# Five sums of the mixture ahead of the turn of raw K in VectorE's written order

## The chip, the cores and the metric

One core of one Trainium2 chip. The metric is the device time of one execution in microseconds; the time of a kernel is the median of its runs. Five engines work side by side, each through its own queue in order: TensorE (PE; its weight loads are shown apart as PEld), VectorE (DVE), ScalarE (ACT), GpSimd (POOL) and SyncE (SP), whose queue starts nearly all transfers.

## What is computed

Two blocks. The first is a recurrence over 768 time steps for 4 batches of 8 heads of dimension 40:

```python
for t in range(S):
    y[:, :, t] = np.einsum('bhd,bhde->bhe', rt, state)
    Sa = np.einsum('bhde,bhe->bhd', state, at)
    state_decay = state * wt[:, :, None, :] - np.einsum('bhd,bhe->bhde', Sa, bt)
    state = state_decay + np.einsum('bhd,bhe->bhde', vt, kt)
```

The second takes y as a matrix x of 3072 x 320 through four experts, with weights `p` normalised over the experts:

```python
for e in range(E):
    h = np.maximum(x @ w1[e], 0.0)
    out += p[:, e:e + 1] * (h @ w2[e])
```

All numbers are fp32; `w1[e]` is 320 x 1024, `w2[e]` 1024 x 320.

## The kernel before

**Units and steps.** Time is cut into 12 chunks of 64 steps, the batches into two pairs, which gives 24 units (`NU`). The main loop (line 1311) runs over `u` from 1 to 23; "step u" below is one pass of it. Three stages of different units overlap in a step: `step` of unit u (the state), `merge` and the first part of `step` for unit u + 1, `within` and `substitute` for unit u + 2.

**The chain of a unit.** `within` turns the raw inputs with VectorE (`turn_raw`, line 324): W into G, A into AT, R into RT, B into NT, K into KT. From unit 8 on (`BY_CHANNEL`), NT and KT are each turned in two halves, noted as `Br` and `Kr`, and then multiplied by `gp`, the reciprocal of the decays (lines 633 to 645; noted as `N` and `K`). NT is read by the matmuls `pfe`, KT by `pe`. `substitute` solves a triangular system: VectorE makes M, GpSimd works through it in the tile Z (lines 760 and 777). `merge` turns Z on VectorE into `Qc` and `QTc` (lines 793, 794), and TensorE then computes `pY` and `pQ`. In `step`, the matmuls `prn`, `psat`, `pxr` and `pdy` follow; VectorE adds Y (line 913) and the states (lines 924, 925) from `pdy`, and SP sends Y into `xT`, the input of the mixture.

**The mixture.** For each chunk of 128 x 2 rows and each expert, `ups` computes `ph = xT . w1` in two halves (`up_last`, `up_main`), and ScalarE writes relu of it into `hs` (line 978). The product with `w2` is done with sums of blocks: `add_h` (line 1096) makes five sums of blocks of `hs`, named a1, a7, a5, a2, a6 and noted as `sum_a0`, `sum_a1` and so on. Each is one VectorE addition of 128 x 512 (line 1104) into a tile of which there is only one. `down_1` computes `p431`: two terms of 8 matmuls from `hs`, a third of 8 from a1. `down_2` computes `p75` (from a7, a5) and `p26` (from a2, a6), 16 matmuls each. VectorE adds each result into `osb` (line 993): `p431` takes four adds, `p75` and `p26` two each. `ph` and the `p` tiles share one pool of three PSUM tiles in turn, so that a `p431` takes the tile that the `p26` before it held.

The pieces of the mixture stand in a list (`todo`), from which `mix` puts some between the parts of each step. In a late step TensorE sees in this order: `p75`, `p26`, `pev`, `pdy`, the start of a `ph`, `p431`, the rest of `ph`, `pg`, `pc`, `pY`, `prn`; later `p75`, `p26`, `pfe`, and `p431`, `pe`, `pxr`.

**What sets the order.** TensorE's order is the order of the program. VectorE's is made by the scheduler under stated dependences that cost no wait (`BEHIND`): the text `VECTOR_ORDER` for the early units, and rules in `ahead_of_merge` (lines 1441 to 1450) for units 8 to 23. A pair `(one, then)` in it means: `then` stands behind `one` on VectorE (line 1453):

```python
for one, then in [*zip(names, names[1:]), ..., *ahead_of_merge]:
    tc.add_manual_dep(made[then].ins, made[one].ins.name, BEHIND, ...)
```

In a late step ten sums are made: five behind the reciprocal `1/gp` (line 1449), and five, `sum_a{10 * (u - 1) - 50}` to the fourth after it, which line 1443 puts behind the multiplies `K` and `N` of unit u. These multiplies belong to the step u - 2; there are sixteen such groups, in steps 6 to 21.

Of the kernel before, what the change touches and what calls it, by code (L numbers as in the profile page):

```python
# [33 lines left out]
def kernel(  # L34
# [48 lines left out]
    NU = NC * B // 2  # L83
# [128 lines left out]
    BY_CHANNEL = 8  # L212
# [1222 lines left out]
    for piece in last:  # L1435
# [4 lines left out]
    waits_of_scalar = [(f"SXc0.{n}", "RTc1.0") for n in range(4)]  # L1440
    ahead_of_merge = [(f"{x}{u}", f"Qc{u - 1}") for u in range(BY_CHANNEL, NU) for x in "KN"]
    ahead_of_merge += [
        (f"{x}{u}", f"sum_a{10 * (u - 1) - 50 + n}") for u in range(BY_CHANNEL, NU) for x in "KN" for n in range(5)
    ]
    ahead_of_merge += [(f"VC{u}.{r}", f"1/gp{u + 1}") for u in range(BY_CHANNEL, NU - 1) for r in range(2)]
    ahead_of_merge += [(f"RH{u - 1}.{r}", f"1/gp{u + 1}") for u in range(BY_CHANNEL, NU - 1) for r in range(2)]
# [37 lines left out]
```

## Time and profile before

| | |
|---|---|
| time, median of 3 runs (lowest to highest) | 1082.37 us (1082.31 to 1082.71) |
| profiled execution, its own time | 1082.07 us |
| its span (first to last instruction) | 1080.3 us |
| TensorE busy / its weight loads | 1053.6 us / 944.2 us |
| VectorE busy | 801.6 us, 1565 instructions |
| GpSimd busy | 527.6 us, 1322 instructions |
| ScalarE busy | 344.2 us, 942 instructions |
| mean granted TensorE clock | 0.998 |

In the rows below, a timeline row gives the start, the duration, the engine, the line, the operation, output<-input, shapes and how many instructions were merged into the row; a bracket gives the idle time of the engine just before it and what ended it. A row of waits reads: who waited, for whom, total us, how many times, the longest.

### The profile page before, as it was taken

The page shows a single profiled execution, that of the slowest core. Times are in us where ns is not written, and L with a number is a line of the kernel's source. Part 1 is how long each engine was busy: PE and PEld are TensorE (multiplying, and loading weights), DVE is VectorE, ACT ScalarE, POOL GpSimd, SP SyncE. Part 2 cuts the span into 40 slices and gives each one's busy share as a digit, 9 for nine tenths or more (in the row PEclk, how much of TensorE's full clock was granted, in tenths as well). Part 3 has the DMA queues.
Part 4 walks back from the last instruction along what each step waited for, and adds up shares of the span by engine and source line. Part 5 has one row for each costly group of instructions (what it writes and reads, how often), then busy time and mean ns, then how long its engine had stood idle before and what let it go on. Part 6 is the DMA issues. An engine that isn't in the chain of part 4 may idle for free.

```text
span 1080.3 us, 38526 instructions
## 1 busy us (share of the span) xinstructions
PE 1053.6 (98%) x16022; PEld 944.2 (87%) x16022; DVE 801.6 (74%) x1565; ACT 344.2 (32%) x942; POOL 527.6 (49%) x1322
## 2 busy tenths in 40 slices
PE   8999999999999999999999999999999999999998
PEld 7888878888889989889989898998988998998887
DVE  7787679898777967978778779778787786634343
ACT  3433344423333323324233333232233333221110
POOL 6117777756465374464563653744735636420000
PEclk9999999999999999999999999999999999999999
DMA  6776644444444443543453353354444443121220
GB/s 119 192 202 140 138 106 112 83 101 106 109 96 109 102 113 74 131 108 78 114 126 82 88 143 71 92 133 88 99 113 101 102 104 86 53 73 51 75 85 13
DMA packets 275350, 111.05 MB, mean 103 GB/s; under 512 B 229816, under 2 KB 254952, under 8 KB 275176
## 3 DMA queue, kind: packets, MB, share of 16 engines
q1 hardware_dynamic: 271192, 107.75, 42.8%
q8 instruction: 126, 2.06, 0.8%
q10 hardware_dynamic: 3984, 0.84, 0.4%
q14 instruction: 48, 0.39, 0.1%
HBM read 100.65 MB, written 3.93 MB: 97 GB/s over the span
## 4 chain that ended last, share of the span: by engine, by line
PE 76%; DVE 10%; POOL 8%; issue 2%; DMA 2%; ACT 1%; SPq 1%; DVEq 0%; POOLq 0%
PE ph L110 33%; PE p L110 25%; POOL Z L777 5%; POOL Z L760 3%; PE pdy L110 2%; DVE a L1104 2%; PE prn L110 2%; PE po L110 2%; PE pxr L110 2%; PE psat L110 2%; PE pfe L110 1%; PE warm L110 1%; PE pc L110 1%; PE pY L110 1%; PE pe L110 1%
## 5 line engine op out<-in xcount | busy, mean ns | idle before, releaser
L777 POOL TENSOR_TENSOR Z<-Z 128x31 f32<-128x31 f32 (+7 forms) x704 | 261.1, 371 | 55.1
L110 PE MATMUL ph<-xT,w1b 128*128 128x256 f32 (+3 forms) x1536 | 222.4, 374 | 0.5 <-issue 0.5
L978 ACT ACTIVATE hs<-ph 128x512 f32<-128x512 f32 (+1 forms) x208 | 117.0, 564 | 331.8 <-PE ph L110 329.8
L110 PE MATMUL ph<-xT,w1a 128*128 128x256 f32 (+3 forms) x1536 | 220.8, 373 | 0.0
L993 DVE SCALAR_TENSOR_TENSOR osb<-p,gate,osb 128x320 f32<-128x320 f32 (+1 forms) x243 | 108.2, 482 | 133.1 <-PE p L110 130.9
L760 POOL TENSOR_TENSOR Z<-M,Z 128x62 f32<-128x62 f32 (+7 forms) x352 | 149.6, 425 | 95.3 <-DVE M L746 69.6
L110 PEld LDWEIGHTS ph<-xT,w1b 128*128 128x128 f32 (+1 forms) x1536 | 168.8, 161 | 27.8 <-issue 7.0
L110 PEld LDWEIGHTS ph<-xT,w1a 128*128 128x128 f32 (+1 forms) x1536 | 167.9, 161 | 28.3 <-issue 6.7
L1104 DVE TENSOR_TENSOR a<-hs 128x512 f32<-128x512 f32 x220 | 148.8, 710 | 41.2 <-ACT hs L978 41.2
L110 PE MATMUL p<-sums,a 128*128 128x160 f32 x1056 | 165.7, 300 | 9.7 <-DVE a L1104 9.7
L110 PEld LDWEIGHTS p<-sums,a 128*128 128x128 f32 x1056 | 152.6, 190 | 13.6 <-DVE a L1104 11.4
L727 POOL COPY below<-F 32x256 f32<-32x256 f32 x48 | 20.6, 430 | 177.4 <-ACT F L670 175.8
L110 PEld LDWEIGHTS p<-w,hs 128*128 128x128 f32 x704 | 98.6, 190 | 9.0 <-issue 7.8
L110 PE MATMUL p<-w,hs 128*128 128x160 f32 x704 | 104.9, 302 | 0.5 <-DVE osb L993 0.5
L110 PE MATMUL p<-w,a 128*128 128x160 f32 x704 | 102.8, 299 | 0.0
L110 PEld LDWEIGHTS p<-w,a 128*128 128x128 f32 x704 | 98.0, 190 | 0.0
L800 POOL COPY QT<-QTc 32x256 f32<-32x256 f32 x96 | 40.3, 420 | 92.6 <-DVE QTc L794 74.9
L898 ACT COPY RS<-pxr 64x256 f32<-64x256 f32 x88 | 32.3, 367 | 104.7 <-DVE SX L499 92.6
L582 DVE RECIPROCAL gp<-G 128x512 f32<-128x512 f32 x16 | 53.6, 3353 | 0.5
L730 DVE STREAM_TRANSPOSE M<-blocks 128x1024 f32<-128x1024 f32 x24 | 47.4, 1975 | 3.3 <-ACT blocks L722 3.0
L708 ACT COPY EV<-pev 64x160 f32<-64x160 f32 x96 | 23.1, 286 | 83.7 <-PE pev L110 83.4
L670 ACT COPY F<-pfe 128x256 f32<-128x256 f32 x48 | 15.5, 376 | 80.1 <-PE pfe L110 77.9
(167 smaller groups left out, 1422.0 us busy)
## 6 DMA issues: line engine op xcount, KB each, us to landing
w1a<-in_moe_w_dram SPq DMA_DIRECT2D x37, 512.0 KB
w1b<-in_moe_w_dram SPq DMA_DIRECT2D x37, 512.0 KB
w<-in_moe_w_dram SPq DMA_DIRECT2D x4, 1280.0 KB
w1a<-in_moe_w_dram SPq DMA_DIRECT2D x74, 64.0 KB
w1b<-in_moe_w_dram SPq DMA_DIRECT2D x74, 64.0 KB
out_dram<-osb SPq DMA_DIRECT2D x45, 80.0 KB
rawW<-in_w_dram SPq DMA_DIRECT2D x48, 72.0 KB
natV<-in_v_dram SPq DMA_DIRECT2D x42, 80.0 KB
```

What stands on the lines that cost most here:

```text
L110: return stated(nc.tensor.matmul(**k))
L582: pin(noted(nc.vector.reciprocal(out=gp[:], in_=G[:, :, 1:L + 1]), "1/gp", q.u))
L708: nc.scalar.copy(out=of_slot(q.EV[half(p)], i ^ p)[:, :, 0:D], in_=pev[i][half(p)])
L727: tc.keep_in_program_order(nc.gpsimd.tensor_copy(out=q.below[quarter(i)], in_=q.F[quarter(i), :, 0:Q]))
L730: ins = nc.vector.transpose(out=M[:], in_=cols)
L760: ins = eng.tensor_tensor(out=Z[:, 1:3, 0:n, j + 1:Q], in0=M[:, j:j + 2, None, j + 1:Q].to_broadcast([P, 2, n, m]), in1=Z[:, here, 0:n, j: ...
L777: eng.tensor_tensor(out=z[:, 0], in0=z[:, 0], in1=z[:, x], op=ALU.add)
L800: ins = nc.gpsimd.tensor_copy(out=q.QT[quarter(i), :, quarter(i % 2)], in_=QTc[quarter(i)])
L898: nc.scalar.copy(out=RS[half(s), x ^ s::2], in_=prs[x][half(s)].rearrange("p (j i) t -> p j i t", i=2),)
L978: ins = nc.scalar.activation(out=h[:, i * HF // 2:(i + 1) * HF // 2, 0:n], in_=ph[i][:], func=ACTF.Relu,)
L993: ins = nc.vector.scalar_tensor_tensor(out=to, in0=p, scalar=sc, in1=to, op0=ALU.mult, op1=ALU.add)
L1104: ins = nc.vector.tensor_tensor(out=t[:], in0=x, in1=y, op=op)
```

## The change

One rule of VectorE's order is replaced. Before, each of the five sums stood behind the multiplies K and N of unit u; now each of them stands ahead of `Kr{u}.0`, the turn of the first half of raw K of unit u. The tie to N is dropped.

```diff
     ahead_of_merge += [
-        (f"{x}{u}", f"sum_a{10 * (u - 1) - 50 + n}") for u in range(BY_CHANNEL, NU) for x in "KN" for n in range(5)
+        (f"sum_a{10 * (u - 1) - 50 + n}", f"Kr{u}.0") for u in range(BY_CHANNEL, NU) for n in range(5)
     ]
```

On TensorE, ScalarE, GpSimd and SP the instructions stand in the same order as before. On VectorE the scheduler's order moves with the rule. In step 9, for one, it was

```
RT turn, osb<-p75 (2), NT turns (2), NT multiply, osb<-p26 (2), Y (2), states and Y, KT turns, KT multiply, a1, a7, a5, a2, a6, osb<-p431 (4)
```

and becomes

```
RT turn, a1, a7, osb<-p75, a5, osb<-p75, a2, NT turn, osb<-p26, a6, osb<-p26, NT turn, NT multiply, Y (2), states and Y, KT turns, KT multiply, osb<-p431 (4)
```

In even steps the sums stand among the `osb` adds in the same way, and the KT turns and multiply come between them and Y, where before the sums came between KT and Y.

## The prediction

> **What bounds the kernel now.** I read the page's first part, then the waits of TensorE (PE) and of its weight loads (PEld) from 322 to 915 us.
>
> ```profile
> span 1080.3 us, 38526 instructions
> PE 1053.6 (98%) x16022; PEld 944.2 (87%) x16022; DVE 801.6 (74%) x1565; ACT 344.2 (32%) x942; POOL 527.6 (49%) x1322
> ...
> PE p L110 <- DVE a L1104: 9.7, 7, 1.4
> PE pY L110 <- DVE QTc L794: 1.0, 3, 0.5
> PE pY L110 <- PE pc L110: 0.7, 3, 0.2
> PE pY L110 <- issue: 0.2, 1, 0.2
> PEld p L110 <- DVE a L1104: 11.4, 7, 1.7
> ```
>
> TensorE is the bound: a change can gain only where TensorE stands still. In this stretch, which holds steps 8 to 21, it does so at two places: seven times before `p` for the A sums (`a`), and seven times before `pY`. The timeline of TensorE in step 8, then in step 9, shows both:
>
> ```profile
> 350.92 2.44 PE L110 MATMUL p<-w,hs 128*128 128x160 f32 x16
> 353.20 1.25 PE L110 MATMUL p<-sums,a 128*128 128x160 f32 x8
> 354.29 3.62 PE L110 MATMUL ph<-xT,w1a 128*128 128x256 f32 x16
> 358.27 0.69 PE L110 MATMUL pc<-RT,VT 40*64 40x64 f32 x32
> 359.18 0.59 PE L110 MATMUL pY<-QTc,below 64*64 64x64 f32 x13 [0.21 <-DVE QTc L794]
> ...
> 392.89 2.44 PE L110 MATMUL p<-w,hs 128*128 128x160 f32 x16
> 396.68 1.35 PE L110 MATMUL p<-sums,a 128*128 128x160 f32 x8 [1.35 <-DVE a L1104]
> 397.87 3.62 PE L110 MATMUL ph<-xT,w1a 128*128 128x256 f32 x16
> 401.85 0.69 PE L110 MATMUL pc<-RT,VT 40*64 40x64 f32 x32
> 402.37 0.57 PE L110 MATMUL pY<-QTc,below 64*64 64x64 f32 x13
> ```
>
> Step 8 goes from the start of `p431` (16 matmuls, then 8 that need sum a1) to the next `ph` in 354.29 - 350.92 = 3.37 us; step 9 takes 397.87 - 392.89 = 4.98. The stall costs 1.61, more than its 1.35 of idle time, because the pipeline fills anew. The weight loads' row gives all seven together: 11.4 us. At `pY` it is the even step that loses: 0.91 us from `pc` to `pY` against 0.52, so 0.39.
>
> The timeline of VectorE in the same two steps shows why:
>
> ```profile
> 345.79 0.55 DVE L993 SCALAR_TENSOR_TENSOR osb<-p,gate,osb 128x320 f32<-128x320 f32 x1 [3.23 <-PE p L110]
> 347.96 0.55 DVE L993 SCALAR_TENSOR_TENSOR osb<-p,gate,osb 128x320 f32<-128x320 f32 x1 [1.20 <-PE p L110]
> 350.25 3.66 DVE L1104 TENSOR_TENSOR a<-hs 128x512 f32<-128x512 f32 x5
> 353.83 0.74 DVE L913 TENSOR_TENSOR Y<-pdy,RS 128x256 f32<-128x256 f32 x2
> ...
> 387.76 0.55 DVE L993 SCALAR_TENSOR_TENSOR osb<-p,gate,osb 128x320 f32<-128x320 f32 x1 [4.16 <-PE p L110]
> 388.35 0.38 DVE L993 SCALAR_TENSOR_TENSOR osb<-p,minus_gate,osb 128x160 f32<-128x160 f32 x1
> 388.65 0.76 DVE L324 STREAM_TRANSPOSE NT<-rawB 128x256 f32<-128x256 f32 x2
> 389.44 0.69 DVE L640 SCALAR_TENSOR_TENSOR NT<-NT,gp 128x512 f32<-128x512 f32 x1
> 392.15 0.76 DVE L913 TENSOR_TENSOR Y<-pdy,RS 128x256 f32<-128x256 f32 x2 [1.13 <-PE pdy L110]
> 395.90 3.19 DVE L1104 TENSOR_TENSOR a<-hs 128x512 f32<-128x512 f32 x5
> 399.02 1.58 DVE L993 SCALAR_TENSOR_TENSOR osb<-p,gate,osb 128x320 f32<-128x320 f32 x4
> ```
>
> VectorE is idle for 3.23 us ahead of 345.79 and 4.16 ahead of 387.76, while work stands queued behind it. In step 9 the K work ends up behind Y and the states, and the sums behind K: they start at 395.90, though `p431` wants the first at 392.89 + (353.20 - 350.92) = 395.17. In step 8 they are in time, but push Y to 353.83 and the chain Y, states, `Qc`, `QTc` into `pY`.
>
> **The change part by part.** No instruction is added or removed; the order on TensorE, ScalarE, GpSimd and SP's queue is the same as before. On VectorE the five sums now stand, in sixteen steps (6 to 21), between and ahead of the four `osb` adds of `p75` and `p26`; K's turns and multiply come behind them.
>
> *The sums' new place.* The sums need `hs`, whose second half ScalarE finishes here, and four of their tiles must have been read by the expert before:
>
> ```profile
> 343.61 0.60 ACT L978 ACTIVATE hs<-ph 128x512 f32<-128x512 f32 x1 [1.13 <-PE ph L110]
> 385.58 0.60 ACT L978 ACTIVATE hs<-ph 128x512 f32<-128x512 f32 x1 [0.76 <-PE ph L110]
> ```
>
> So sums can begin at 344.21 and 386.18. At 3.66/5 = 0.73 each, the first two are done at 345.67 and 387.64, inside the idle time, and the first `osb` add starts no later. The others alternate with the adds, by when `p75` and `p26` have read their tiles. Hence a1 is ready some 8 us ahead of 395.17 and the stall goes whole: **-11.4 us**. If only its visible idle time came back: -9.7; if a1 were still late, 0.
>
> *What is behind the sums in step 9.* From 387.76: add 0.55, sum 0.73, add 0.38, sum 0.73, half of the NT turns 0.38, add 0.55, sum 0.73, add 0.38 end at 392.19. That frees the PSUM tile of `p26`, which `p431` takes at 392.89: 0.7 to spare (in step 8, 349.84 against 350.92). Then 0.38 + 0.69 of NT: Y starts at 393.26 at the latest, 1.1 later than now. Behind Y come 395.90 - 392.15 = 3.75 of states and K (till 397.01) and the four adds (1.58, till 398.6); nothing of it is wanted by TensorE before `pY`. The send of Y to xT on SP's queue is up to 1.1 later too; its reader is the next chunk's first `ph`, behind the next `p75`, `p26` and `pfe`, and no row shows TensorE waiting for xT. K's multiply is for `pe` of the next step. Cost: 0; without this room, at most 1.1 x 7 = 7.7.
>
> *Step 8.* From 345.79 the same sum of durations, with the second add of full width not ahead of 347.96, ends at 349.84; K's 0.76 and 0.69 follow, so Y starts near 351.3 instead of 353.83. `Qc` and `QTc` then wait for GpSimd and not for VectorE.
>
> *GpSimd, the cover of all this.* `pY` also needs the substitution Z. Its rows (GpSimd's timeline, and TensorE's for the one step in which Z alone set `pY`):
>
> ```profile
> 273.64 0.51 POOL L777 TENSOR_TENSOR Z<-Z 128x8 f32<-128x8 f32 x2
> 275.43 0.59 PE L110 MATMUL pY<-QTc,below 64*64 64x64 f32 x13 [1.47 <-DVE QTc L794]
> 350.63 1.31 POOL L777 TENSOR_TENSOR Z<-Z 128x49 f32<-128x49 f32 x2
> 355.88 0.52 POOL L777 TENSOR_TENSOR Z<-Z 128x8 f32<-128x8 f32 x2
> 392.49 0.66 POOL L777 TENSOR_TENSOR Z<-Z 128x49 f32<-128x49 f32 x2
> 396.79 1.16 POOL L777 TENSOR_TENSOR Z<-Z 128x8 f32<-128x8 f32 x2
> L1104 DVE TENSOR_TENSOR a<-hs x165: 627/683/890, 240.9 to 925.3; 128x512 f32<-128x512 f32 x165
> ```
>
> From Z's end to `pY`, with nothing else late, it takes 275.43 - 274.15 = 1.28. Today step 8 has 359.18 - 356.40 = 2.78, step 9 has 402.37 - 397.95 = 4.42. Without the lost time: 2.78 - 0.39 - 1.28 = 1.11 to spare in step 8, 4.42 - 1.61 - 1.28 = 1.53 in step 9. Beside the sums GpSimd runs at half speed (two adds of 49 columns: 1.31 at 350.63, 0.66 at 392.49), so five sums cost Z 3.66/2 = 1.83. In step 8 they lay beside Z before and do so after: no change. In step 9 only the part from 395.90 to Z's end at 397.95 did, 2.05/2 = 1.03; now all do, and Z ends 0.80 later. 0.73 is left. I take 0, and the even steps get back seven times what they wait: idle 1.0 + 0.7 + 0.2 = 1.9, and with the refill that makes 0.21 idle into 0.39 lost, 0.18 x 7 more: **-3.1 us**. The ends: 0 (the wait stays), and a loss worked out below.
>
> The Trainium skill (SBUF — State Buffer, section Who interferes with whom) speaks against the change: a VectorE instruction with two SBUF inputs contends with a GpSimd one that reads SBUF, and whichever issues second blocks fully till the other ends. The two rows of 49 columns agree in kind. By a full block for each sum the time would be the first rival's, 1077.3; by the measured half speed it is 1067.9.
>
> *The sum.* Profiled execution: 1082.07, of which the span is 1080.3. 1082.07 - 11.4 - 3.1 = 1067.6. The median of the runs, 1082.37, lies 0.3 higher: **1067.9 us**.
>
> **The rivals.**
> 1. *A wait for Z takes the place of the wait for a1.* For: the two 49-column rows. Against: the 0.73 and 1.11 to spare. If GpSimd loses each sum's whole median, 5 x 0.683 = 3.42, Z is 2.39 later in step 9, 0.86 beyond its 1.53; in step 8 1.59 later, 0.48 beyond. The gain shrinks by 7 x (0.86 + 0.48) = 9.4: 1077.3. Smaller losses lie between.
> 2. *The even steps keep their wait,* because Y's chain comes no sooner. Against: VectorE's idle 3.23 us. 1071.0.
> 3. *The change does not do what it says:* the first sums wait for `hs` until the `osb` adds are ready, and the queue moves along behind them. Against: 344.21 and 386.18. About 1082.4.
> 4. *Slower: GpSimd becomes the bound in every step.* Place: Z's end, deciding from 1.53 us (odd) and 1.11 (even). If a sum blocks GpSimd for the longest row, 0.890, five take 4.45: odd steps then wait 4.45 - 1.03 - 1.53 = 1.89 where 1.61 is saved, even ones 4.45 - 1.83 - 1.11 = 1.51 where 0.39 is: 7 x (0.28 + 1.12) = 9.8 more, 1092.2. Against: with five sums in full beside it, step 8 kept 2.78.
>
> **How the numbers follow.** Forecast 0.78, rivals 0.10, 0.05, 0.03, 0.04. The forecast's own range is 1066.0 (one stall's worth, 1.6 us, gained besides in steps 6 and 7, which lie outside the stretch) to 1070.5 (nearly all of the even steps' 3.1 us stays); with 0.22 left for the rivals, I take it up to 1075, past rival 2 and into rival 1. What a measurement can tell from no change is 0.2%, 2.2 us. Faster: the forecast, rivals 1 and 2, so 0.93; rival 3 gives 0.03 within; rival 4 gives 0.04 slower.
>
> **What would show it.** Right: TensorE's row for `p` waiting for `a` is gone between 322 and 915 us; `p431` to `ph` takes 3.4 us in odd steps too; VectorE's idle time ahead of the first `osb` add falls from 3 to 4 us to below 1; Y starts 2 to 3 us sooner in even steps, up to 1.1 later in odd ones; Z ends 0.5 to 1 us later in odd steps, measured from `pfe`. Wrong: rows of `pY` waiting for `QTc`, with `Qc` waiting for Z, above 0.3 us in each step (rivals 1 and 4), a wait of `p` for `osb` (the PSUM tile of `p26`), or a1 still starting behind the adds (rival 3).

## The result, and the profile after

| | before | after |
|---|---|---|
| time, median (lowest to highest), 4 runs each | 1082.34 us (1081.73 to 1082.71) | 1066.78 us (1066.64 to 1067.89) |
| ratio, with its 95% interval | | 0.9859 (0.9842 to 0.9876) |
| profiled execution, its own time | 1082.07 us | 1067.89 us |

The kernel became 1.4% faster; the forecast was 1067.9 us. The profiled execution of after is 1.0 to 1.25 us slower than its three other runs, and the trace shows where: it reaches step 6 late (below). The head of the page after:

```profile
span 1066.1 us, 38525 instructions
PE 1049.8 (98%) x16022; PEld 942.5 (88%) x16022; DVE 802.2 (75%) x1565; ACT 344.2 (32%) x942; POOL 538.8 (51%) x1322
...
L1104 DVE TENSOR_TENSOR a<-hs 128x512 f32<-128x512 f32 x220 | 155.3, 724 | 81.8 <-ACT hs L978 81.8
```

GpSimd is busy 11.2 us longer (527.6 before). VectorE's idle time ahead of the sums, which ends with ScalarE's `hs`, is 81.8 us, where it was 41.2; its idle time ahead of the `osb` adds fell from 133.1 to 69.4.

From 322 to 915 us TensorE has no row of waits left. Of the waits of `p`'s weight loads one row is left, the same as before and for nothing that the profile shows:

```profile
PEld p L110 <- issue: 5.4, 14, 0.4
```

`p` waiting for `a` is gone, and so is `pY` waiting for `QTc`. TensorE's timeline in steps 8 and 9:

```profile
351.69 2.44 PE L110 MATMUL p<-w,hs 128*128 128x160 f32 x16
...
355.05 3.62 PE L110 MATMUL ph<-xT,w1a 128*128 128x256 f32 x16
...
359.03 0.69 PE L110 MATMUL pc<-RT,VT 40*64 40x64 f32 x32
359.55 0.57 PE L110 MATMUL pY<-QTc,below 64*64 64x64 f32 x13
...
393.22 2.44 PE L110 MATMUL p<-w,hs 128*128 128x160 f32 x16
...
396.58 3.62 PE L110 MATMUL ph<-xT,w1a 128*128 128x256 f32 x16
...
400.56 0.69 PE L110 MATMUL pc<-RT,VT 40*64 40x64 f32 x32
401.08 0.57 PE L110 MATMUL pY<-QTc,below 64*64 64x64 f32 x13
```

Both steps now run alike: 3.36 us from `p431` to `ph`, 0.52 from `pc` to `pY`. From `pc` to `pc` the step takes 400.56 - 359.03 = 41.53 us, where it was 401.85 - 358.27 = 43.58.

To account for the whole gain, here are TensorE's `pc` rows in step 5, in step 6 (after: with its `pY`) and in step 21; first before:

```profile
230.64 0.69 PE L110 MATMUL pc<-RT,VT 40*64 40x64 f32 x32 [0.61 <-DVE RT L324]
...
273.26 0.69 PE L110 MATMUL pc<-RT,VT 40*64 40x64 f32 x32
...
913.38 0.69 PE L110 MATMUL pc<-RT,VT 40*64 40x64 f32 x32
```

and after:

```profile
231.92 0.69 PE L110 MATMUL pc<-RT,VT 40*64 40x64 f32 x32 [1.25 <-DVE RT L324]
...
274.54 0.69 PE L110 MATMUL pc<-RT,VT 40*64 40x64 f32 x32
...
276.43 0.59 PE L110 MATMUL pY<-QTc,below 64*64 64x64 f32 x13 [1.19 <-DVE QTc L794]
...
899.18 0.69 PE L110 MATMUL pc<-RT,VT 40*64 40x64 f32 x32
```

- Up to `pc` of step 6, the profiled execution of after loses 274.54 - 273.26 = 1.28 us, all of it by `pc` of step 5 (231.92 - 230.64), ahead of the first moved sum, which stands in step 6. The three other runs are faster by about as much. In the traces of the kernels below this `pc` of step 6 starts anywhere from 272.45 us (the first sum alone) to 278.14 (no rule at all), so it varies from one execution to the next and is not the change's doing.
- From step 6 to step 8: (358.27 - 273.26) - (359.03 - 274.54) = 0.52 gained.
- From step 8 to step 21: (913.38 - 358.27) - (899.18 - 359.03) = 14.96 gained.
- From there to the end of the span: 1080.3 - 913.38 = 166.9 and 1066.1 - 899.18 = 166.9, nothing.

0.52 + 14.96 = 15.48, which is the difference of the medians (15.56); less 1.28 it is the difference of the spans (14.2).

VectorE's timeline in the two steps (of the rows between, those of the other sums, of NT, of K and of the rest of `osb` are left out):

```profile
345.01 1.69 DVE L1104 TENSOR_TENSOR a<-hs 128x512 f32<-128x512 f32 x2 [1.68 <-ACT hs L978]
346.62 0.54 DVE L993 SCALAR_TENSOR_TENSOR osb<-p,gate,osb 128x320 f32<-128x320 f32 x1
...
351.53 0.75 DVE L913 TENSOR_TENSOR Y<-pdy,RS 128x256 f32<-128x256 f32 x2
...
386.54 1.55 DVE L1104 TENSOR_TENSOR a<-hs 128x512 f32<-128x512 f32 x2 [2.62 <-ACT hs L978]
...
391.74 0.37 DVE L993 SCALAR_TENSOR_TENSOR osb<-p,minus_gate,osb 128x160 f32<-128x160 f32 x1
...
393.35 0.74 DVE L913 TENSOR_TENSOR Y<-pdy,RS 128x256 f32<-128x256 f32 x2
```

Two sums fill the idle time that stood ahead of the first `osb` add, and that add follows them without a gap. To set these times against those of before, take off what the two traces are apart at `p431`: 351.69 - 350.92 = 0.77 in step 8, 393.22 - 392.89 = 0.33 in step 9.

GpSimd's timeline after, in steps 8, 9 and 10, at the places that matter:

```profile
345.37 0.78 POOL L760 TENSOR_TENSOR Z<-M,Z 128x150 f32<-128x150 f32 x1
346.23 1.10 POOL L777 TENSOR_TENSOR Z<-Z 128x75 f32<-128x75 f32 x2
347.40 0.75 POOL L760 TENSOR_TENSOR Z<-M,Z 128x130 f32<-128x130 f32 x1
348.23 1.13 POOL L777 TENSOR_TENSOR Z<-Z 128x65 f32<-128x65 f32 x2
349.44 0.76 POOL L760 TENSOR_TENSOR Z<-M,Z 128x132 f32<-128x132 f32 x1
...
356.81 0.51 POOL L777 TENSOR_TENSOR Z<-Z 128x8 f32<-128x8 f32 x2
...
386.58 0.97 POOL L760 TENSOR_TENSOR Z<-M,Z 128x150 f32<-128x150 f32 x1
...
398.33 0.51 POOL L777 TENSOR_TENSOR Z<-Z 128x8 f32<-128x8 f32 x2
...
428.10 0.99 POOL L760 TENSOR_TENSOR Z<-M,Z 128x150 f32<-128x150 f32 x1
...
430.34 0.96 POOL L760 TENSOR_TENSOR Z<-M,Z 128x130 f32<-128x130 f32 x1
...
440.33 0.52 POOL L777 TENSOR_TENSOR Z<-Z 128x8 f32<-128x8 f32 x2
```

`pY` starts at 359.55 and 401.08 (above), and in step 10 at 442.62, so that Z ends 2.23 us ahead of `pY` in step 8, 2.24 in step 9 and 442.62 - 440.85 = 1.77 in step 10. 1.28 is needed, so 0.95, 0.96 and 0.49 us are to spare. The other even steps up to 20 read as step 10 does; the other odd steps have 0.79 to 0.96.

### The profile page after: what moved, and what is told of

The parts are those of the page before. It is cut to its first block, busy times and chain, and to the rows that moved or that the text cites. A ratio compares the mean times of both kernels' runs of the same rounds, so it can differ in the third digit from the quotient of the medians.

```text
span 1066.1 us, 38525 instructions
## 1 busy us (share of the span) xinstructions
PE 1049.8 (98%) x16022; PEld 942.5 (88%) x16022; DVE 802.2 (75%) x1565; ACT 344.2 (32%) x942; POOL 538.8 (51%) x1322
## 4 chain that ended last, share of the span: by engine, by line
PE 81%; POOL 8%; DVE 5%; issue 2%; DMA 2%; SPq 1%; ACT 1%; DVEq 0%; POOLq 0%; ACTq 0%
PE ph L110 36%; PE p L110 29%; POOL Z L777 5%; POOL Z L760 3%; PE pdy L110 3%; PE prn L110 2%; PE po L110 2%; PE pxr L110 2%; PE psat L110 2%; PE pfe L110 1%; PE pc L110 1%; DVE M L730 1%; PE pev L110 1%; PE pe L110 1%; PE pQ L110 1%
## 5 line engine op out<-in xcount | busy, mean ns | idle before, releaser
L777 POOL TENSOR_TENSOR Z<-Z 128x31 f32<-128x31 f32 (+7 forms) x704 | 265.6, 377 | 55.1
L1104 DVE TENSOR_TENSOR a<-hs 128x512 f32<-128x512 f32 x220 | 155.3, 724 | 81.8 <-ACT hs L978 81.8
L760 POOL TENSOR_TENSOR Z<-M,Z 128x62 f32<-128x62 f32 (+7 forms) x352 | 155.9, 443 | 94.9 <-DVE M L746 69.1
L993 DVE SCALAR_TENSOR_TENSOR osb<-p,gate,osb 128x320 f32<-128x320 f32 (+1 forms) x243 | 107.6, 480 | 69.4 <-PE p L110 66.2
```

The source lines that it names most:

```text
L760: ins = eng.tensor_tensor(out=Z[:, 1:3, 0:n, j + 1:Q], in0=M[:, j:j + 2, None, j + 1:Q].to_broadcast([P, 2, n, m]), in1=Z[:, here, 0:n, j: ...
L777: eng.tensor_tensor(out=z[:, 0], in0=z[:, 0], in1=z[:, x], op=ALU.add)
L993: ins = nc.vector.scalar_tensor_tensor(out=to, in0=p, scalar=sc, in1=to, op0=ALU.mult, op1=ALU.add)
L1104: ins = nc.vector.tensor_tensor(out=t[:], in0=x, in1=y, op=op)
```

## The experiments

All kernels were timed in three rounds against the kernel before on the same chip, whose medians there were 1082.05 us (the first four kernels), 1081.82 (the next two) and 1082.84 (the last). Edits are shown against the changed kernel.

**The odd steps alone.** The new rule for odd steps, the old one for even.

```diff
-        (f"sum_a{10 * (u - 1) - 50 + n}", f"Kr{u}.0") for u in range(BY_CHANNEL, NU) for n in range(5)
+        (f"sum_a{10 * (u - 1) - 50 + n}", f"Kr{u}.0") for u in range(BY_CHANNEL, NU) for n in range(5) if u % 2 == 1
+    ]
+    ahead_of_merge += [
+        (f"{x}{u}", f"sum_a{10 * (u - 1) - 50 + n}") for u in range(BY_CHANNEL, NU) for x in "KN" for n in range(5) if not (u % 2 == 1)
```

> The new rule stands for odd units alone (odd steps 7 to 21), the old one for even units (steps 6 to 20). My theory: the gain is two separate ones, about 11.5 us from the seven stalls of p before a1 in odd steps and 3.4 us from the seven waits of pY in even steps. Then the stalls are gone, pY keeps waiting 0.4 to 0.8 us in even steps, and the time is 1082.3 - 11.8 = 1070.5 us. Rival: the even steps' wait is only an echo of the stalled step before it; then nearly the whole gain is here, 1067, and pY waits no more.

Measured: 1070.23 us (1069.36 to 1071.18), ratio 0.9887 (0.9872 to 0.9902). TensorE's waits in the stretch hold no `p`, and `pY` still waits in even steps, where it starts 0.84 to 1.00 us after `pc`; the two largest rows are:

```profile
PE pY L110 <- PE pc L110: 0.7, 3, 0.2
PE pY L110 <- DVE QTc L794: 0.5, 2, 0.3
```

So the even wait is not an echo of the odd stall: it stays when the stall goes.

**The even steps alone.** The same edit with the two conditions exchanged.

```diff
+        (f"sum_a{10 * (u - 1) - 50 + n}", f"Kr{u}.0") for u in range(BY_CHANNEL, NU) for n in range(5) if u % 2 == 0
```

> The new rule stands for even units alone (even steps 6 to 20), the old one for odd units. My theory: only the 3.4 us of pY in even steps and some 0.3 of step 6 come back: 1078.6 us, with the seven stalls of p before a1, 1.6 us each, still there. Rival (the even wait is an echo of the stall): no gain, 1082.3.

Measured: 1077.96 us (1077.53 to 1080.77), ratio 0.9957 (0.9940 to 0.9974). The stalls of `p` remain, `pY` waits no more:

```profile
PE p L110 <- DVE a L1104: 9.4, 7, 1.3
```

The two halves gain 1082.05 - 1070.23 = 11.8 and 1082.05 - 1077.96 = 4.1 us, together 15.9; the whole change gained 15.6. Within the intervals, 1.6 and 1.8 us to either side, they add up.

**The first sum alone.** Only a1 ahead of the turn of raw K; the other four stay behind K and N.

```diff
+        (f"sum_a{10 * (u - 1) - 50 + n}", f"Kr{u}.0") for u in range(BY_CHANNEL, NU) for n in range(5) if n == 0
+    ]
+    ahead_of_merge += [
+        (f"{x}{u}", f"sum_a{10 * (u - 1) - 50 + n}") for u in range(BY_CHANNEL, NU) for x in "KN" for n in range(5) if not (n == 0)
```

> Of each five sums only a1 goes ahead of the turn of raw K; the other four stay behind the multiplies K and N. Theory A (a1 is what TensorE stands for, and in even steps 0.7 us of sums less ahead of Y is enough to free pY, which waits 0.4): the stalls are gone, pY waits in no step but 6 and perhaps 14, 1066.8 us. Theory B (the even steps' gain needs all five sums out of the way of Y): stalls gone, pY still waiting 0.3 to 0.4 in even steps, 1069.5 to 1070.5. If a1 alone were not enough for p, the time would stay near 1082.

Measured: 1070.14 us (1069.31 to 1070.67), ratio 0.9885 (0.9871 to 0.9900). The number is that of the theory by which even steps keep their wait, but the reason is another: even steps are free (0.51 to 0.52 us from `pc` to `pY`), and it is the odd ones that wait. VectorE's timeline in step 9 of this kernel:

```profile
394.37 2.68 DVE L1104 TENSOR_TENSOR a<-hs 128x512 f32<-128x512 f32 x4
...
398.47 0.61 DVE L793 STREAM_TRANSPOSE Qc<-Z 128x256 f32<-128x256 f32 x1
399.12 0.45 DVE L794 STREAM_TRANSPOSE QTc<-Qc 128x256 f32<-128x256 f32 x1
```

and TensorE's:

```profile
398.82 0.69 PE L110 MATMUL pc<-RT,VT 40*64 40x64 f32 x32
399.71 0.59 PE L110 MATMUL pY<-QTc,below 64*64 64x64 f32 x13 [0.20 <-PE pc L110]
```

`Qc` has no bracket: it does not wait for Z but for VectorE's own queue, where four sums (2.68 us) stand ahead of the adds. `QTc` ends at 399.57, `pY` starts 0.89 us after `pc`. Before the change the stall of `p` hid this: it held `pY` back by 1.61 us, in which VectorE got through. So a1 alone ends the stalls, but with the other four left where they were the next wait in the same queue comes up, some 0.4 us in each odd step.

**No rule at all.** The old rule is taken out and none put in.

```diff
     ahead_of_merge += [
-        (f"sum_a{10 * (u - 1) - 50 + n}", f"Kr{u}.0") for u in range(BY_CHANNEL, NU) for n in range(5)
     ]
```

> The old rule is taken away and the new one is not put in: the scheduler is free. The order on VectorE is that of the changed kernel from step 7 on and differs in step 6 alone, where K's second turn and multiply stand among the sums. My theory: the gain comes from taking the tie of the sums to K and N away, so 1066.8 us within 0.5. Rival: the new rule matters through step 6, whose Z decides pY there: then up to 1.5 us either way, 1065.3 to 1068.3.

Measured: 1067.83 us (1066.51 to 1071.8), ratio 0.9871 (0.9848 to 0.9894), within its spread the time of the change. The scheduler then places the sums as the new rule does from step 7 on. Its profiled execution is the slowest of the four, but lost its time ahead of step 6: from `pc` of step 8 to that of step 21 it takes 903.11 - 362.92 = 540.19 us, the changed kernel 899.18 - 359.03 = 540.15. In step 6, where the orders differ, `pY` starts 2.17 us after `pc` instead of 1.89. So nearly the whole gain lies in lifting the old tie to K and N; the new one is worth some 0.3 us in step 6.

**One, then three more copies on GpSimd.** How near is Z, the cover of the whole change? To Z's chain a copy of a constant into a part of Z that nobody reads is added, once or three times a step (three are shown), output unchanged:

```diff
                 for x in range(1, 3):
                     eng.tensor_tensor(out=z[:, 0], in0=z[:, 0], in1=z[:, x], op=ALU.add)
+                if j == 14 and q.u >= 10:
+                    for _ in range(3):
+                        tc.keep_in_program_order(eng.tensor_copy(out=Z[:, 3], in_=unit_cols[:]))
```

> The changed kernel with one more copy of one column on GpSimd (about 0.40 us and 0.07 us to the next instruction) at the end of Z's chain in steps 8 to 21, output unchanged. It asks how much room the change has left between Z and pY. Theory from the changed kernel's trace: Z ends 1.77 us ahead of pY in even steps and 2.2 us in odd ones, and Qc, QTc and the way to pY need 1.28 us, so 0.49 us is spare at the least: one copy fits, 1066.8 us (+-0.5), and pY begins 0.52 us after pc in every step. Rival (the spare of even steps is already used up because the wait for Qc also ends with VectorE's own work): +0.4 us in each of seven even steps, 1069.6 us.

> The changed kernel with three such copies (about 1.41 us in all) in steps 8 to 21, output unchanged. Theory from the changed kernel's trace (spare 0.49 us in even steps, 0.94 us in odd ones): pY waits 0.92 us in each of seven even steps and 0.47 us in each of seven odd ones, 9.7 us in all, 1076.5 us; the page of waits then has pY waiting for Z. Rival by the prediction's own spares (1.11 us even, 0.73 us odd): 0.30 and 0.68 us, 6.9 us in all, 1073.7 us, and the odd steps wait longer than the even ones. Rival that Z is not what comes next (pY depends on VectorE's own order alone): 1066.8 us.

Measured: 1066.86 us (1066.62 to 1067.26), ratio 0.9855 (0.9835 to 0.9875) with one copy, and 1072.37 us (1072.05 to 1072.46), ratio 0.9905 (0.9881 to 0.9928) with three. The first is as the theory said, the second missed both figures. The copies ran in steps 9 to 22, and in the middle of the chain, not at its end: in places beside VectorE's sums. There a copy's time is not what it adds. From Z's first multiply to its end, one copy added 0.13 us in step 9 and nothing in step 10 (0.11 less); three added 1.34 and 0.63. With three, `pY` started 0.91 us after `pc` in step 9 and 0.67 in step 10, 0.39 and 0.16 more than without; so the room was 1.34 - 0.39 = 0.95 and 0.63 - 0.16 = 0.47 us, which is what the trace after gave. That odd steps waited longer than even ones, as the rival by the prediction's own spares had it, comes from the larger push that they got here; the room is the larger in odd steps. The size of the push was wrong, not that of the room.

**Three copies where no sum runs.** The same, with `j == 28` in place of 14:

```diff
-                if j == 14 and q.u >= 10:
+                if j == 28 and q.u >= 10:
```

> The changed kernel with three more copies of one column on GpSimd in steps 9 to 22, output unchanged, now among the last operations of Z's chain (behind the adds of 24 columns and between those of 8), where VectorE runs no sums. The first copy of such a kind put the next operation back by 0.21 us (1.04 us from the adds of 68 columns to the next multiply in place of 0.83, in the kernel with one copy); for the others about 0.3 us each, so Z ends some 0.8 us later in every step. Theory (room 0.49 us in even steps, 0.94 us in odd ones): even steps lose about 0.3 us at pY, odd steps nothing; seven even steps and step 22 make about 2.5 us, 1069.3 us. Rival by the prediction's own figures (1.11 us even, 0.73 us odd): even steps lose nothing and odd ones about 0.1 us, 1067.5 us. If each copy cost its whole 0.47 us, Z would end 1.4 us later, both would lose (0.9 and 0.5 us) and the time would be near 1076.5 us.

Measured: 1068.99 us (1067.82 to 1072.51), ratio 0.9887 (0.9866 to 0.9908). The runs spread too far for the time alone to tell the theory (1069.3) from the rival (1067.5); the trace can. GpSimd's timeline at Z's end in steps 9 and 10 of this kernel:

```profile
397.78 0.22 POOL L777 TENSOR_TENSOR Z<-Z 128x8 f32<-128x8 f32 x1
...
439.76 0.22 POOL L777 TENSOR_TENSOR Z<-Z 128x8 f32<-128x8 f32 x1
```

VectorE's, waiting for it in step 10:

```profile
440.02 0.63 DVE L796 STREAM_TRANSPOSE Qc<-Z 128x256 f32<-128x256 f32 x1 [1.61 <-POOL Z L777]
```

and TensorE's:

```profile
399.06 0.69 PE L110 MATMUL pc<-RT,VT 40*64 40x64 f32 x32
399.57 0.57 PE L110 MATMUL pY<-QTc,below 64*64 64x64 f32 x13
...
440.60 0.69 PE L110 MATMUL pc<-RT,VT 40*64 40x64 f32 x32
441.28 0.59 PE L110 MATMUL pY<-QTc,below 64*64 64x64 f32 x13
```

In step 9, Z's end stands 399.57 - 398.00 = 1.57 us ahead of `pY`, 0.67 less than after, and `pY` is on time (0.51). In step 10 it stands 441.28 - 439.98 = 1.30 ahead, all that is needed, and `pY` is 0.68 behind `pc`: 0.16 late. All even steps from 10 on read so (0.67 to 0.69), and no odd one does. The even steps then lose 0.2 rather than the 0.3 us expected, since Z's end moved by 0.65 and not by 0.8: from `pc` to the next `pc`, step 10 takes 41.74 us against 41.53 to 41.54, so that a `pY` 0.16 us late costs 0.04 more behind it. From `pc` of step 8 to that of step 21 the kernel takes 898.92 - 357.52 = 541.40 us, 1.25 more than after, about 0.2 in each of the six even steps from 10 to 20. Hence the even steps from 10 on are the tight ones, with 0.49 us of room, and not the odd ones.

## Why the prediction was right

**The bound.** Right: TensorE lost time at two places, and both rows are gone. All that was gained was gained there.

**-11.4 us, the stalls of `p`.** Right. From `p431` of each odd step to that of the step after it, the profiled executions are 1.65, 1.58, 1.70, 1.65, 1.69, 1.62 and 1.64 us shorter, 11.53 in all; in step 9, 1.62 lies between `p431` and `ph` (4.98 to 3.36), so it is the stall with its refill and not its idle 1.35 alone. The odd steps alone gave 11.8.

**-3.1 us, `pY` in even steps.** Right, slightly small: 14.96 - 11.53 leaves 3.43. The seven times from `pc` to `pY` shrank by 3.1 as forecast (six from about 0.92, step 14 from 1.22, to about 0.52); the 0.3 more is about what a late `pY` costs behind it, if the 0.04 a step of the last experiment, where it was 0.16 us late, hold for 0.4 too.

**What the sum left out.** Steps 6 and 7, which it counted at nothing, gave 0.52 us: step 6's `pY` waits 1.19 us for `QTc` in place of 1.47, and in step 7 it starts 0.51 in place of 0.70 us after `pc`. The 0.3 and 0.5 are most of the 1.1 us between 1067.9 and 1066.8.

**The sums in VectorE's idle time.** Right. Less the 0.77 and 0.33 us that the traces are apart, the sums start at 344.24 and 386.21, against 344.21 and 386.18. Y starts at 350.76 in step 8, 3.07 sooner than before (near 351.3 was forecast), and at 393.02 in step 9, 0.87 later (at most 1.1). The PSUM tile of `p26` is read by 392.11, 1.11 us ahead of `p431` at 393.22, where 0.7 was expected.

**GpSimd.** Here one term was fair and one step failed, without harm. In step 9, Z was to end 0.80 us later. From the multiply of 150 columns to Z's end it took 397.95 - 386.24 = 11.71 before (GpSimd's row below) and takes 398.84 - 386.58 = 12.26 after, 0.55 later. From Z's first multiply to its end the seven odd steps lose 0.55 to 1.18 (step 17: 21.28 to 22.46), 0.9 in the mean.

```profile
386.24 0.45 POOL L760 TENSOR_TENSOR Z<-M,Z 128x150 f32<-128x150 f32 x1
386.77 0.77 POOL L777 TENSOR_TENSOR Z<-Z 128x75 f32<-128x75 f32 x2
387.61 0.42 POOL L760 TENSOR_TENSOR Z<-M,Z 128x130 f32<-128x130 f32 x1
388.11 0.75 POOL L777 TENSOR_TENSOR Z<-Z 128x65 f32<-128x65 f32 x2
388.94 0.43 POOL L760 TENSOR_TENSOR Z<-M,Z 128x132 f32<-128x132 f32 x1
```

"In step 8 they lay beside Z before and do so after: no change" is the step that failed. Z's chain lengthens by 0.18 us in step 8 (22.25 to 22.43 from its first multiply to its end) and by about 0.6 in steps 10 to 20 (22.34 to 22.90 in step 10), so that 0.49 us of the 1.11 is left. The five sums do lie beside Z in both kernels, but not beside the same instructions of it. In step 10 they put it back by 0.33 us each before, 1.65 in all; after, by 0.54, 0.33, 0.54, 0.40 and 0.33, which is 2.14. The two of 0.54 are those beside the multiplies of 150 and 130 columns (0.99 and 0.96 us above, against 0.45 and 0.42 here). The room that the prediction called the smaller, 0.73 in odd steps, is the larger, 0.96 in step 9. The last experiment shows this with the wait that comes when the room is used up.

**The rivals.** The first, a wait for Z in place of the wait for a1, was the near one: one half microsecond more on Z and it begins, as the copies showed, though its price is small at first (0.16 us in each even step of the last kernel). The second, even steps that keep their wait, is the state that the odd steps alone show, 1070.23 against its 1071.0; in the changed kernel Y comes 3.07 us sooner and the wait is gone. The third falls with the times of the sums. The fourth, GpSimd as the bound, needed Z to be 1.11 us later in even steps or 1.53 in odd ones; it came 0.6 and at most 1.18 later.

The Trainium skill (SBUF — State Buffer, section Who interferes with whom) has the second instruction to issue block fully till the first ends. The trace agrees that the two engines hold each other up; a full block for each sum, as the first rival priced it (Z 2.39 us later in step 9), did not come: it was 0.55 there and 1.18 at the most in other odd steps. What a sum costs (0.32 to 0.56 us, below) is about half to four fifths of its own 0.68; that would fit a block which begins within a sum, but no run here tells it from other causes.

## What to carry to other kernels

Where the bound engine waits for a short instruction of another, look at what stands ahead of it in that engine's queue and at the idle time ahead of that; work whose inputs are early belongs into the idle time. Ask next what the same queue holds for the next wait: moving the first sum alone ended one wait and left another. And where a second engine works beside the moved instructions, its room must be measured in every kind of step, best by adding work to it until the bound engine waits.

## What the runs showed of the hardware

What the prediction read as half speed is a loss counted by VectorE's instructions: each sum holds up one instruction of GpSimd, once. In step 8 after, the five sums run from 345.01 to 349.91 us. Beside them five instructions of GpSimd take longer than the same ones in step 9 before, where no sum runs beside them (both above): by 0.33 us the multiply of 150 columns, one of the two adds of 75, the multiply of 130 and the multiply of 132, and by 0.38 one of the two adds of 65. That is 1.70 for five sums; the prediction's half speed had 1.83.

The count holds over the whole stretch. From 330 to 915 us of the trace after, 126 VectorE instructions of 128 x 512 that read two tiles, neither of them in PSUM, run beside Z's chain: the sums, the multiplies of NT, KT and AT, and that of Y by G. Beside them 126 of Z's instructions, of 31 to 150 columns, lose 0.32 to 0.57 us each. Seven more lose 0.18 to 0.19, each beside the multiply of a state (128 x 160); the 438 that have none of these beside them, but at most `osb` adds, turns and the like, lose 0.02 at the most. Before, instructions as small as 16 columns lost 0.33 as well (0.56 us instead of 0.23 in step 9), so the loss does not go by size. Why some lose 0.33 and others 0.54 stays open.

A copy that nothing waits for costs GpSimd's chain less than its duration: three copies of 0.40 us each between Z's last operations moved Z's end by 0.67 us in step 9. GpSimd's timeline of that kernel, in step 10, shows that such an instruction begins before the one ahead of it has ended: the adds of 24 columns end at 438.43, the copy at 438.77.

```profile
437.87 0.56 POOL L777 TENSOR_TENSOR Z<-Z 128x24 f32<-128x24 f32 x2
438.37 0.40 POOL L780 COPY Z<-unit_cols 128x256 f32<-128x256 f32 x1
438.73 0.23 POOL L760 TENSOR_TENSOR Z<-M,Z 128x16 f32<-128x16 f32 x1
```
